# A new order of steps for a fused attention and gated-MLP kernel: two sink exponentials in place of four, two gate tiles begun on half their contraction, and a last tile in halves

## The chip, the cores and the metric

The kernel runs on one core of one Trainium2 chip. The metric is the device time of one execution in microseconds: the median of eight runs of the unchanged kernel, and one more execution under the hardware profiler, from which all lines of profile below come. A core has five engines that run side by side and wait for one another by semaphores: PE (matrix multiply; its weight loads are listed as PEld), DVE (vector), ACT (scalar, with function tables), POOL (GpSimd) and SP (which here only issues transfers). Sixteen DMA engines move data.

## What is computed

Attention with a window of 128 and four sink positions, for 4 batches, 8 heads, 768 positions and 64 dimensions a head; then a gated MLP on the result, with a spatial projection over positions.

```python
scores = scale * np.matmul(q, k.transpose(0, 1, 3, 2))
keep = is_sink | in_window          # pos < 4, or 0 <= row - col < 128
a = softmax(np.where(keep, scores, -1e9))
x = heads_joined(np.matmul(a, v))   # (4, 768, 512)
h = gelu_tanh(x @ w_in)             # (4, 768, 1024)
u, v = h[..., :512], h[..., 512:]
v_n = (v - mean(v)) / np.sqrt(var(v) + 1e-06) * g_ln
v_s = np.einsum('ts,bsd->btd', w_sg, v_n) + b_sg[None, :, None]
out = x + (u * v_s) @ w_out
```

Inputs and output are float32; inside, matrices are bf16 and sums float32.

## The kernel before

Everything is written out as one list of steps by hand, the string STEPS. A step is a name and indices, and the program calls the function of that name; each function issues instructions on fixed engines, and an engine takes its own in the order of the list. There is no scheduler at run time: an instruction that waits holds all that is behind it on its engine. The first index is the batch b. Heads go in pairs p (0 to 3), the 768 positions in six tiles of 128 (t or j).

The steps of attention, with their lines in the kernel before:

- LQ, LK, LV load q, k, v. Pair 0 of batch 0 comes over SP in float32 (`first`, L200) and is cast by CQ and CK (L221); all other loads are issued by POOL (L192, L214), cast on the way. Batch 3's q and k come in rows (L196, two transfers a step) and are turned by transposing DMAs of SP.
- TQ, TK turn q and k of a pair on PE (L300, twelve transposes); EQ, EK copy the result out of PSUM (L219 on ACT, L221 on DVE; the step's last letter names the engine).
- QK.b.p.g computes scores of group g (0 to 2) of a pair (L350), EX their exponential on ACT (L358; 128x1024, or 128x768 for g = 2), MK masks it, on DVE (L365) or in two instructions on POOL (L369, L373).
- KS, SK, SX make the sinks' scores and their exponential (L323, L332 and L336, L341). In batch 0 one SK and one SX are done for each pair, elsewhere one SX for the batch.
- AV.b.p.h averages v for one half h of the positions, tiles 0 to 2 or 3 to 5 (L390 to L400), NR divides by the sum (L409, L410 on DVE). VSM prepares the sinks' v (L288, L289); its data come by LC, four small transfers of SP.
- XT.b.i transposes x (L419; i selects a half of the positions and of the columns: XT.0.0 and XT.0.2 need pairs 0 and 1, XT.0.1 and XT.0.3 pairs 2 and 3), XE copies it out. Batches 2 and 3 use a transposing DMA instead (XD).

The steps of the MLP: MV.b.jj makes two tiles of the value half (L436, eight matmuls over four contraction blocks c), GV its gelu (L440), BN the statistics (L449, L450, L452), RS the power -1/2 on POOL (L457), NM and Z the normalised tile z (L460; L466 on ACT, L469 on DVE). MU.b.i and GU do the gate half (L478, L484). WT and WE turn the spatial weights once (L491, L494); LW loads w_in in two halves, LWS the spatial weights, LWO w_out. SP.b.h.dc is the spatial projection (L499; the step, not the engine), GT adds bias and scale (L504, DVE), GM multiplies by the gate (L509, DVE or POOL). OU.b.t is one output tile (L516, 128x512), RA adds x (L520, DVE), ST stores it (L523, issued by SP). HM.n puts n matmuls without use ahead of the next step on PE[...].

Buffers are rings that a step takes in turn: two score buffers in PSUM shared by QK, MV and MU; four PSUM banks shared by all other PE steps, so that such a step waits for the reader of the fourth one before it; three output tiles ot; three buffers vt. The MLP of a batch is interleaved with the attention of the next. POOL's transfers use eight semaphores in turn: each waits for the landing of the eighth before it.

Of the kernel before, what the change touches and what calls it, by code (L numbers as in the profile page):

```python
# [16 lines left out]
ZERO LQ.0.0 IDEN LK.0.0 LQ.0.1 FILL LK.0.1 LC VSK MASK LV.0.0 MASK0 CQ.0.0.D LQ.0.2 HM.7 TQ.0.0 CK.0.0.D LK.0.2  # L17
EQ.0.0.A TK.0.0 LV.0.1 EK.0.0.A TQ.0.1 KS.0.0 QK.0.0.2 LQ.0.3 EQ.0.1.D QK.0.0.0 EX.0.0.2 SK.0.0 LK.0.3 VSM.0 TK.0.1
LV.0.2 EK.0.1.D SX.0.0 QK.0.0.1 MK.0.0.2.P EX.0.0.0 HM.1 TQ.0.2 KS.0.1 LV.0.3 EX.0.0.1 MK.0.0.0 SK.0.1 QK.0.1.2 LW.0
TK.0.2 EQ.0.2.D SX.0.1 QK.0.1.1 EX.0.1.2 EK.0.2.D MK.0.0.1.P EX.0.1.1 QK.0.1.0 MK.0.1.2.D LW.1 HM.1 AV.0.0.0 EX.0.1.0  # L20
KS.0.2 QK.0.2.1 MK.0.1.1.D TQ.0.3 LWS EX.0.2.1 QK.0.2.0 MK.0.1.0 AV.0.1.1 LWO EX.0.2.0 NR.0.0.0 AV.0.1.0 QK.0.2.2
NR.0.1.1 TK.0.3 EQ.0.3.A MK.0.2.1.P NR.0.1.0 EK.0.3.A SK.0.2 LQ.1.0 AV.0.0.1 MK.0.2.0 SX.0.2 XT.0.0 KS.0.3 LK.1.0
EX.0.2.2 NR.0.0.1 QK.0.3.0 AV.0.2.0 LV.1.0 EX.0.3.0 XE.0.0.D QK.0.3.1 XT.0.2 MK.0.2.2.D EX.0.3.1 SK.0.3 LV.1.1
MK.0.3.0 QK.0.3.2 AV.0.2.1 NR.0.2.0 SX.0.3 MK.0.3.1.P EX.0.3.2 NR.0.2.1 XE.0.2.A LQ.1.1 MK.0.3.2.D HM.1 AV.0.3.0
NR.0.3.0 LK.1.1 AV.0.3.1 LV.1.2 NR.0.3.1 XT.0.1 XE.0.1.A HM.1 XT.0.3 LV.1.3 XE.0.3.D MV.0.0 VSM.1 VSM.3 MV.0.2 GV.0.0
VSM.2 LG WT.3 WT.1 GV.0.2 WE.3 MV.0.1 BN.0.0 MU.0.3 GV.0.1 BN.0.2 WT.2 GU.0.3 MU.0.2 BN.0.1 RS.0.2 WT.4 GU.0.2 WT.5
MU.0.0 NM.0.2 RS.0.1 WE.1 Z.0.5.A WE.2 Z.0.4.A TQ.1.1 WE.4 TQ.1.0 NM.0.1 GU.0.0 WE.5 TK.1.0 LQ.2.0 MU.0.1 Z.0.3.D
Z.0.0.A Z.0.2.D EQ.1.1.A Z.0.1.D WT.0 EQ.1.0.D GU.0.1 SP.0.1.0 EK.1.0.D SP.0.1.2 GT.0.1.0 WE.0 QK.1.0.2 GM.0.1.0.P
# [36 lines left out]

HOLDS = "LG<LWS"


DT = (3,)


@with_exitstack
def kernel(
    ctx: ExitStack,
    tc: tile.TileContext,
# [12 lines left out]
    nc = tc.nc  # L90
# [482 lines left out]
```

## Time and profile before

| | us |
|---|---|
| median of 8 runs | 160.94 |
| lowest and highest run | 160.38, 162.25 |
| the profiled execution | 162.19 |
| its span on the core | 160.5 |
| PE idle before its first instruction | 2.29 |
| first transposes of q on PE | 5.77 |
| first value tile of batch 0 (L436) | 26.97 |
| last matmul ends | 155.81 |

The span is what the profile covers; some 1.7 us of the execution lie around it. Table rows from 2.29 on are read from the timeline, in microseconds from the span's start.

The busy time of each engine in eleven stretches of the span, as the profile sums it (a pair of numbers is busy time and count of instructions; PEclk is the granted clock of PE):

```profile
core 0: us, PE busy (x) PEld busy (x) DVE busy (x) ACT busy (x) POOL busy (x), PEclk, DMA share, GB/s
0.00:6.00 6.00, 3.38 (x13) 1.20 (x15) 3.33 (x16) 1.28 (x1) 5.12 (x14) 1.00 0.72 173
6.00:16.00 10.00, 7.23 (x111) 4.32 (x107) 7.05 (x13) 7.41 (x10) 10.00 (x14) 0.86 1.74 166
16.00:28.00 12.00, 10.53 (x176) 7.04 (x175) 10.36 (x27) 10.57 (x14) 8.36 (x12) 0.97 1.27 206
28.00:42.00 14.00, 14.00 (x133) 8.83 (x132) 12.51 (x32) 10.01 (x13) 4.75 (x5) 1.00 1.54 202
42.00:70.00 28.00, 27.97 (x425) 17.60 (x422) 26.91 (x56) 23.39 (x29) 23.88 (x33) 1.00 1.46 149
70.00:86.00 16.00, 15.28 (x118) 8.32 (x117) 13.78 (x32) 12.48 (x14) 13.92 (x17) 1.00 1.97 179
...
144.00:156.00 12.00, 11.81 (x65) 6.12 (x63) 8.96 (x17) 0.12 (x1) 3.64 (x4) 1.00 0.24 89
156.00:160.50 4.50, 0.00 (x0) 0.00 (x0) 1.18 (x2) 0.00 (x0) 0.00 (x0) 0.95 0.47 175
```

A busy PE is not a PE at its peak, since the ends of pipelined matmuls are modelled. In the stretch from 42 to 70 us four engines are busy for over four fifths of the time; in the last 4.5 us only DVE and the store's transfer work.

### The profile page before, as it was taken

The page shows a single profiled execution, that of the slowest core. Times are in us where ns is not written, and L with a number is a line of the kernel's source. Part 1 is how long each engine was busy: PE and PEld are TensorE (multiplying, and loading weights), DVE is VectorE, ACT ScalarE, POOL GpSimd, SP SyncE. Part 2 cuts the span into 40 slices and gives each one's busy share as a digit, 9 for nine tenths or more (in the row PEclk, how much of TensorE's full clock was granted, in tenths as well). Part 3 has the DMA queues.
Part 4 walks back from the last instruction along what each step waited for, and adds up shares of the span by engine and source line. Part 5 has one row for each costly group of instructions (what it writes and reads, how often), then busy time and mean ns, then how long its engine had stood idle before and what let it go on. Part 6 is the DMA issues. An engine that isn't in the chain of part 4 may idle for free.

```text
span 160.5 us, 3815 instructions
## 1 busy us (share of the span) xinstructions
PE 148.2 (92%) x1519; PEld 86.3 (54%) x1519; DVE 133.2 (83%) x304; ACT 100.9 (63%) x118; POOL 88.9 (55%) x123
## 2 busy tenths in 40 slices
PE   4749997999999999999989999999999999999980
PEld 1325664566565667734655655545756654556530
DVE  4469897699999999998789989779999945887861
ACT  3387997549869869976887749746897024580000
POOL 7999784244257999999992680404045420214400
PEclk9996999999999999999999999999999999999999
DMA  5999999999972999999999989410300890111055
GB/s 172 168 161 172 199 213 206 204 222 185 176 105 17 173 194 273 140 138 119 234 172 191 165 155 179 131 65 0 135 0 0 133 263 0 65 70 63 4 198 196
DMA packets 63122, 22.70 MB, mean 141 GB/s; under 512 B 51456, under 2 KB 59904, under 8 KB 63104
## 3 DMA queue, kind: packets, MB, share of 16 engines
q0 software_dynamic: 45600, 11.80, 76.6%
q1 hardware_dynamic: 17504, 10.66, 27.5%
q8 instruction: 12, 0.20, 0.5%
q14 instruction: 6, 0.05, 0.1%
HBM read 24.81 MB, written 6.29 MB: 194 GB/s over the span
## 4 chain that ended last, share of the span: by engine, by line
PE 75%; POOL 6%; ACT 6%; DVE 4%; DMA 4%; issue 1%; POOLq 0%; DVEq 0%; ACTq 0%
PE mm L499 20%; PE mm L516 11%; PE sc L436 11%; PE sc L478 10%; PE sc L350 7%; PE mm L300 5%; DMA q<-in_q_dram 4%; PE mm L390 3%; ACT P L358 3%; PE mm L396 2%; PE mm L400 2%; DVE z L469 2%; PE mm L419 1%; PE mm L491 1%; POOL v_sb L214 1%
## 5 line engine op out<-in xcount | busy, mean ns | idle before, releaser
L358 ACT ACTIVATE P<-sc 128x1024 bf16<-128x1024 f32 (+1 forms) x48 | 43.9, 959 | 9.1 <-PE sc L350 9.0
L499 PE MATMUL mm<-wsgT,z 128*128 128x384 bf16 x192 | 34.7, 327 | 0.7 <-DVE z L469 0.7
L499 PEld LDWEIGHTS <-z 128*128 128x128 bf16 x192 | 17.6, 98 | 13.4 <-issue 2.1
L509 POOL TENSOR_TENSOR wsg_gated<-gtmp,uT 128x384 bf16<-128x384 bf16 x15 | 14.1, 947 | 18.1 <-DVE gtmp L504 18.1
L478 PE MATMUL sc<-xT,w_in_sb 128*128 128x384 bf16 x128 | 23.1, 326 | 0.0
L516 PE MATMUL mm<-w_out_sb,wsg_gated 128*128 128x512 bf16 x96 | 22.7, 379 | 0.0
L369 POOL TENSOR_SCALAR_AFFINE_SELECT P<-P 128x512 bf16<-128x512 bf16 x20 | 13.3, 663 | 16.4 <-ACT P L358 16.3
L436 PE MATMUL sc<-w_in_sb,xT 128*128 128x512 bf16 x96 | 22.0, 379 | 0.0
L504 DVE SCALAR_TENSOR_TENSOR gtmp<-mm,g_sb,b_bc 128x384 bf16<-128x384 f32 x32 | 19.4, 612 | 2.4 <-PE mm L499 2.3
L365 DVE TENSOR_TENSOR P<-P,mask 128x1024 bf16<-128x1024 bf16 (+1 forms) x28 | 20.8, 756 | 0.4 <-ACT P L358 0.2
L520 DVE TENSOR_TENSOR ot<-mm,x_sb 128x512 f32<-128x512 f32 x24 | 16.1, 686 | 5.0 <-PE mm L516 4.7
L449 DVE BATCH_NORM_STATS2 st<-vt 128x6 f32<-128x512 f32 x24 | 16.2, 673 | 4.7 <-ACT vt L440 4.7
L214 POOL DMA_DIRECT2D v_sb<-in_v_dram x16 | 16.5, 1038 | 5.4 <-DMA wsg_gated<-in_moe_w_sg_dram 4.3
L484 ACT ACTIVATE uT<-sc 128x768 bf16<-128x768 f32 x16 | 12.7, 802 | 10.1 <-PE sc L478 10.1
L440 ACT ACTIVATE vt<-sc 128x1024 f32<-128x1024 f32 x12 | 12.3, 1023 | 10.5 <-PE sc L436 10.5
L410 DVE TENSOR_TENSOR x_sb<-mm,rcp 128x384 bf16<-128x384 f32 x32 | 17.8, 558 | 1.1
L390 PE MATMUL mm<-v_sb,P 128*128 128x65 bf16 x192 | 17.2, 196 | 0.7 <-ACT xT L219 0.6
L457 POOL TENSOR_TENSOR rs<-rs,neg_half 128x2 f32<-128x2 f32 (+1 forms) x8 | 7.0, 875 | 18.4 <-DVE rs L452 15.7
L390 PEld LDWEIGHTS <-P 128*128 128x128 bf16 x192 | 14.8, 99 | 4.4 <-issue 2.6
L350 PE MATMUL sc<-qT,kT 64*128 64x256 bf16 x192 | 16.3, 272 | 0.8 <-ACT kT L219 0.8
L478 PEld LDWEIGHTS <-w_in_sb 128*128 128x128 bf16 x128 | 12.3, 98 | 8.5
L396 PE MATMUL mm<-v_sb,P 128*128 128x65 bf16 x160 | 16.0, 195 | 0.0
(73 smaller groups left out, 231.0 us busy)
## 6 DMA issues: line engine op xcount, KB each, us to landing
out_dram<-ot SPq DMA_DIRECT2D x24, 256.0 KB, 2.4
v_sb<-in_v_dram POOLq DMA_DIRECT2D x16, 192.0 KB, 8.2
q<-in_q_dram POOLq DMA_DIRECT2D x4, 384.0 KB, 12.5
k<-in_k_dram POOLq DMA_DIRECT2D x4, 384.0 KB, 11.9
wsg_gated<-in_moe_w_sg_dram POOLq DMA_DIRECT2D x1, 1152.0 KB, 14.1
w_in_sb<-in_moe_w_in_dram POOLq DMA_DIRECT2D x2, 512.0 KB, 9.0
qn<-in_q_dram POOLq DMA_DIRECT2D x8, 96.0 KB, 6.9
kn<-in_k_dram POOLq DMA_DIRECT2D x8, 96.0 KB, 6.5
```

Of the source, the lines that this page charges most:

```text
L214: return nc.gpsimd.dma_start(out=v_sb[b % len(v_sb)][:, 2 * p:2 * p + 2, :, 0:Dh].rearrange("p h t d -> p (h t) d"), in_=v[b, 2 * p:2 * p ...
L350: nc.tensor.matmul(sc[:, hl, 256 * jl:256 * jl + n], kT[b, p][rows, 128 * j:128 * (j + 1)], qT[b, p][rows, 128 * j:128 * j + n], start=Tru ...
L358: nc.scalar.activation(out=pt[:, :, 0:w], in_=sc_ring[b, p, g][:, :, 0:w], func=AF.Exp, scale=scale)
L365: nc.vector.tensor_mul(pt[:, :, 0:w], pt[:, :, 0:w], m.unsqueeze(1).to_broadcast([128, 2, w]))
L390: nc.tensor.matmul(av[:, il, hl, :], P[b, p, i // 2][:, hl, 256 * (i % 2):256 * (i % 2) + 128], vb[:, h, i, :], start=first, stop=False)
L396: nc.tensor.matmul(av[:, il, hl, :], P[b, p, j // 2][:, hl, 256 * (j % 2) + 128:256 * (j % 2) + 256], vb[:, h, j, :], start=False, stop=False)
L410: nc.vector.tensor_mul(xs[:, 3 * half:3 * half + 3, 128 * p:128 * (p + 1)].rearrange("p t (h d) -> p t h d", h=2), av[:, :, :, 0:Dh], rcp. ...
L436: nc.tensor.matmul(hp[:, jl, :], xT[b][:, j, c, :], w_in_sb[:, c, d_half:2 * d_half], start=(c == 0), stop=(c == KD - 1))
L478: nc.tensor.matmul(hp[:, n, 0:NH], w_in_sb[:, c, 128 * dc:128 * (dc + 1)], xT[b][:, 3 * hf:3 * hf + 3, c, :], start=(c == 0), stop=(c == K ...
L499: nc.tensor.matmul(ps[:, 0:NH], z[b][:, si, 128 * dc:128 * (dc + 1)], wsgT[:, si, NH * hf:NH * (hf + 1)], start=(si == 0), stop=(si == NT ...
L504: nc.vector.scalar_tensor_tensor(out=gtmp.new((b, hf, dc)), in0=mm_ring["g", b, hf, dc][:, 0:NH], scalar=g_sb[:, dc:dc + 1], in1=b_bc[:, N ...
L516: nc.tensor.matmul(ps, gatedT[:, (2 * b + hf) % 3, dc, 128 * tl:128 * (tl + 1)], w_out_sb[:, dc, :], start=(dc == 0), stop=(dc == KU - 1))
```

## The change

1. In batch 0 the sinks of two pairs are put into one bank (two SK matmuls, the second adding to the first), so SX is done for pairs 0 and 1 together (SX.0.1) and for 2 and 3 (SX.0.3).
2. MV.0.0 and MU.0.0 are each split over the contraction: MA.0.0 and UA.0.0 do its first two blocks, which need pairs 0 and 1 alone; the rest follows under the old name.
3. q and k of pair 2 of batch 0 are loaded ahead of the first v, pair 3 behind one v in place of two. The casts CQ and CK move from DVE to ACT. The first q and k land in vt buffers; the ring f32 goes, and the rings qT and kT grow from six to eight.
4. Output tile 5 of batch 3 is made, added and stored in two halves of 256 columns (OU, RA, ST, then OB, RB, SB).
5. The whole list of steps is another one: other orders on every engine, and other engines for some masks, copies and products. The functions also gain forms that this list does not use (a turn by rows on PE, TURN "R"; a WE by DMA).

| batch: instruction | before, by engine | after |
|---|---|---|
| 0: masks MK | DVE 8, POOL 4 | DVE 9, POOL 3 |
| 1: masks MK | DVE 7, POOL 5 | DVE 9, POOL 3 |
| 1 and 2: copies EQ | ACT 3, DVE 5 | ACT 6, DVE 2 |
| 0 and 1: copies XE | ACT 4, DVE 4 | ACT 2, DVE 6 |
| 1: products GM | DVE 4, POOL 4 | DVE 5, POOL 3 |
| 2: z | ACT 2, DVE 4 | ACT 1, DVE 5 |
| 3: products GM | DVE 4, POOL 4 | DVE 2, POOL 6 |
| all: HM matmuls | 11 | 10 |

```diff
-    f32 = Ring("f32", 2, [128, 2, NT, Dh], F32)
-    qT = Ring("qT", 6, [128, S], BF16)
-    kT = Ring("kT", 6, [128, S], BF16)
+    qT = Ring("qT", 8, [128, S], BF16)
+    kT = Ring("kT", 8, [128, S], BF16)
...
     def SK(b, p0):
-        ps = fresh(mm_ring, ("s", b, p0))
         ks = ks_sink[b % 2]
         if b == 0:
-            nc.tensor.matmul(ps, ks[:, 128 * p0:128 * (p0 + 1)], qT[b, p0][:, 256:768], start=True, stop=True)
+            ps = mm_ring["s", b, p0 - 1] if p0 % 2 else fresh(mm_ring, ("s", b, p0))
+            nc.tensor.matmul(ps, ks[:, 128 * p0:128 * (p0 + 1)], qT[b, p0][:, 256:768],
+                             start=(p0 % 2 == 0), stop=(p0 % 2 == 1))
             return
...
-        e = exs[b, 0 if b else p]
+        e = exs[b, 0 if b else p | 1]
...
+    def MA(b, jj):
+        fresh(sc_ring, ("v", b, jj))
+        v_part(b, jj, range(KD // 2))
+
+    def MV(b, jj):
+        if ("v", b, jj) in sc_ring.held:
+            return v_part(b, jj, range(KD // 2, KD))
+        fresh(sc_ring, ("v", b, jj))
+        v_part(b, jj, range(KD))
...
+    def UA(b, i):
+        fresh(sc_ring, ("u", b, i))
+        u_part(b, i, range(KD // 2))
...
+    def cols_of(b, t, second=False):
+        n = d_model // 2 if b == B - 1 and t in LAST else d_model
+        return slice(n, 2 * n) if second else slice(0, n)
...
+    def OB(b, t):
+        o_part(b, t, cols_of(b, t, True))
```

The order in the places that the prediction speaks of, before and after. POOL at the start:

```diff
-LQ.0.1 LK.0.1 VSK MASK LV.0.0 LQ.0.2 LK.0.2 LV.0.1 LQ.0.3 LK.0.3 LV.0.2 MK.0.0.2.P LV.0.3 LW.0 MK.0.0.1.P LW.1 LWS LWO
+LQ.0.1 LK.0.1 MASK LQ.0.2 VSK LK.0.2 LV.0.0 LQ.0.3 LK.0.3 LV.0.1 LV.0.2 LV.0.3 LW.0 LW.1 LWS LWO
```

PE at the end of the first batch:

```diff
-AV.0.2.1 AV.0.3.0 AV.0.3.1 XT.0.1 XT.0.3 MV.0.0 MV.0.2 WT.3 WT.1 MV.0.1
+AV.0.3.0 AV.0.2.0 XT.0.2 MA.0.0 AV.0.3.1 XT.0.1 AV.0.2.1 UA.0.0 MV.0.0 MU.0.0 XT.0.3 MV.0.1 WT.3 WT.5
```

POOL around the powers of batch 1:

```diff
-LK.3.0 LV.3.0 MK.2.0.2.P LQ.3.1 LK.3.1 LV.3.1 MK.2.1.2.P LQ.3.2 RS.1.2 LK.3.2 LV.3.2 LQ.3.3 RS.1.1 LK.3.3 LV.3.3
+LQ.3.0 LK.3.0 LV.3.0 MK.1.3.1.P LQ.3.1 MK.1.2.1.P MK.2.0.1.P LK.3.1 MK.2.0.2.P MK.2.1.1.P LV.3.1 LQ.3.2 LK.3.2 LV.3.2 LQ.3.3 RS.1.2 LK.3.3 LV.3.3 RS.1.1
```

PE at the end:

```diff
-SP.3.0.1 SP.3.1.1 SP.3.0.0 SP.3.0.3 SP.3.1.0 SP.3.0.2 SP.3.1.2 SP.3.1.3 OU.3.1 OU.3.2 OU.3.0 OU.3.4 OU.3.3 OU.3.5
+SP.3.0.3 SP.3.0.0 SP.3.0.1 SP.3.1.2 SP.3.0.2 SP.3.1.3 SP.3.1.0 OU.3.0 OU.3.1 SP.3.1.1 OU.3.2 OU.3.5 OU.3.3 OB.3.5 OU.3.4
```

## The prediction, made before the changed kernel ran

> **What bounds the kernel now.** First the page: busy times, then the forty slices (4.01 us each), then the chain.
>
> ```profile
> PE 148.2 (92%) x1519; PEld 86.3 (54%) x1519; DVE 133.2 (83%) x304; ACT 100.9 (63%) x118; POOL 88.9 (55%) x123
> PE   4749997999999999999989999999999999999980
> DVE  4469897699999999998789989779999945887861
> DMA  5999999999972999999999989410300890111055
> ```
>
> TensorE is the bound from slice 8 (28 us) to slice 39 (156 us). Before that it waits, and only there and at the end can much be won. DVE is as full between 40 and 73 us. The DMA engines are full until 44 us. Busy PE time is modelled at its ends, so I price PE steps from start to start in the chain: a value tile (L436) 1.73 us, a gate tile (L478) 1.30, a spatial tile (L499, six matmuls) 0.97, an output tile (L516) 0.86. Comparing each step's start-to-start time with the quickest quarter of its kind, PE loses 3.9 us in all after 27 us: 2.1 between 42 and 70 us, 1.1 between 70 and 86 us (0.9 of it one wait at SP.1.1.3, 83.2 us), some 0.7 later.
>
> Next the timeline of the first batch (start, duration, operation, idle time before it and what ended it).
>
> ```profile
> 9.76 1.95 ACT L358 ACTIVATE P<-sc 128x1024 bf16<-128x1024 f32 x2
> 12.99 0.60 ACT L341 ACTIVATE exs<-mm 128x512 bf16<-128x512 f32 x1 [1.28 <-PE mm L332]
> 10.48 0.93 DVE L289 TENSOR_TENSOR v_sink<-vs,headsel 128x512 bf16<-128x512 f32 x1 [1.18 <-DMA vs<-in_v_dram]
> 12.10 0.36 PEld L300 LDWEIGHTS <-q 128*64 128x64 bf16 x12 [2.23 <-DMA q<-in_q_dram]
> 23.41 0.88 ACT L358 ACTIVATE P<-sc 128x768 bf16<-128x768 f32 x1
> 26.97 3.40 PE L436 MATMUL sc<-w_in_sb,xT 128*128 128x512 bf16 x15
> ```
>
> ACT has one long stop (11.71 to 12.99 us), then runs nearly without one until the last exponential ends at 24.29; the last masks, averages, divisions and transposes follow it, and the first value tile starts at 26.97. The third q pair lands only at 12.1 us; its queue had one v load ahead of it.
>
> Third, the chain of waits around 70 to 86 us, and the end.
>
> ```profile
> 75.36 0.72 POOL rs L457
> 76.08 1.68 POOL kn L196 x2
> 77.76 1.01 POOL v_sb L214
> 78.78 1.64 POOL qn L196 x2
> 80.42 1.07 POOL rs L457
> 81.50 0.17 DVE nmr L460
> 81.70 2.68 DVE z L469 x3
> ...
> 142.83 7.80 PE mm L499 x48
> 150.63 5.19 PE mm L516 x24
> ```
>
> The second power of batch 1 stands on POOL behind five loads' issues; its z are late, and SP.1.1.3 waits. The end is eight spatial tiles and six output tiles with no gap; the last two additions (DVE L520, 0.69 each) follow, and the last store.
>
> [...] the same 128x1024 mask takes 0.68 us, or 1.11 (at 51.08) under POOL's work. [...]
>
> **The change part by part.**
>
> Two sink exponentials go: 2 x 0.49 us (start to start, 19.95 to 20.44) on ACT, about 1.0. But CQ and CK come to ACT. They are unseen there: below by DVE's 0.70[...]; I take 0.80. They run at 3.85 and 5.6 us, when q and k land (3.83, 5.58) and ACT is idle until 6.64, so they cost nothing; DVE is rid of 1.5 us.
>
> I walked the new order through the first batch with these rows. EK.0.0 starts at about 7.05, the first exponential at 8.6 as before. VSM.0 still stands on DVE ahead of EK.0.1 and still waits for the 10.4 us landing, so EK.0.1 ends at 12.3 and the next exponential starts at 12.75: ACT stops for 2.2 us here, not 1.28. From there ACT has six wide exponentials (0.92), four narrow (0.70), two sink ones, two copies and XE.0.2: 5.5+2.8+1.0+1.4+0.7 = 11.4. It is never starved in my walk if q.3 lands by 15 us (15.3 before; with two v loads behind it, about 13.8), so the last exponential ends near 23.3 instead of 24.29. The v loads come later (the last near 19.4) but AV.0.3.0 is first asked for at 22.2.
>
> MA (half of 1.73 = 0.86) and UA (half of 1.30 = 0.65) need half 0 of pairs 0 and 1 only, and the weights, landed at 21.34 and 23.88. They run at about 23.6 and 25.9, where PE would wait for the divisions of pairs 2 and 3. The second half of MV.0.0 then starts at 26.55, with 1.51 us done in advance and only XT.0.3 (0.35) still open. Before stood there at 26.97 with nothing done: 26.97 - 26.55 + 1.51 - 0.35 = 1.6 us gained. An unmodelled slip of 0.3 (contention, landings) leaves 1.3. The warm-up matmul less (0.2) lies in waiting time. What is late next: batch 1's first q landed at 35.17 and nothing ahead of it in the queue shrinks; PE arrives there near 34.9. So not much more can be kept.
>
> Batch 1, 40 to 67 us. EQ moves from DVE to ACT three times (0.86 off DVE, 0.70 on ACT each), two masks come from POOL to DVE (0.61 each), XE and a product join DVE. Summed over the list from GT.0.1.0 to the last mask of batch 2's first pairs, DVE has 25.4 us where before had 26.3 (which took 29.9 with contention); ACT has 23.5 for 22.3. POOL has two masks less, but LQ.3.0, LK.3.0 and LV.3.0 (1.65+1.65+1.03) stand ahead of MK.1.3.1: it ends near 57.7, AV.1.3.0 is asked for at 57.9. Each buffer of the ring of four is free in time in my walk, and PE loses 0.35 us where it lost 2.1: 1.7 gained. DVE's contention was 3 us; the walk has only 1.5 us of DVE idleness to hide it, so I give back 0.9 and take 0.8.
>
> The z of batch 1. From MV.1.0 the new PE order has 3x1.73+4x1.30+3x0.86 and 2.5 us of averages and scores before SP.1.1.0: 15.4 us. LQ.3.2 to LQ.3.3 are issued before the first power; the second still has LK.3.3 and LV.3.3 ahead (1.65+1.03). BN.1.1 ends about 11.0 after MV.1.0 starts, the power at 13.1, the last z at 14.9, or 15.4 with DVE under contention (the three took 2.68 against 1.6). That just fits, so most of the 0.9 goes: I take 0.4.
>
> Stages of batch 2 and 3 up to 143 us have the same work and the wait that could open (XD.3.1, landed 3 us ahead before) has 1.6 us left: nothing.
>
> The end. SP.3.1.1 now stands last, behind OU.3.0 and OU.3.1, with its product on POOL. Before, SP.3.1.3 ended at 150.63, its GT at 151.36 and its product (POOL) at 152.35: with 0.06 to PE 1.78 us, under three output tiles (2.6). Now OU.3.2 (0.86) and one half-width matmul (0.11) cover it: a stop of 0.81. Against that, RA.3.4 no longer waits behind RA.3.5: one addition (0.69) after the last matmul, not two. Tail: 157.18 - 142.83 = 14.35 before; 13.0 + 0.81 + 0.73 = 14.5: +0.2. Halving tile 5 shortens nothing that ends last.
>
> Sum: -1.3 - 0.8 - 0.4 + 0.2 = -2.3 us. The profiled execution took 162.19 (span 160.5, 1.7 around it): about 159.9, span 158.2. It lies 1.25 above the median; on the median of 160.94 the forecast is 158.6.
>
> **The rivals.**
>
> DVE stays the second bound: batch 1 waits as before and the z too. For it: its row of nines from 40 to 73, and masks at 1.1 us. Against: 0.9 us less on its list. Gain 1.3 - 0.2 = 1.1: 159.8.
>
> The transfers set the start: batch 1's q and k land no earlier, so a PE that arrives earlier waits at TQ.1.0, or LV.0.0 and q.3 come later than I take and hold AV.0.0.0 and TQ.0.3. For it: the DMA row, and only 0.3 us between arrival and landing. Against: before lost nothing there. First batch gains 0, the rest 1.0: 159.9. Both rivals at once, so that only the end counts: about 161.
>
> Slower: ACT becomes the bound of batch 1. The place is its two score buffers: MV.1.0 needs EX.2.1.2. ACT's list up to it is 21.4 us from 42.0, which gives 63.4; PE comes at 65.1 if it never waits. In before, ACT idled 4.5 us in this stretch, waiting for scores between copies. My forecast has MV.1.0 at about 66.7 (40.0 for the first spatial tile, 25.8 of work and stops, 0.9 given back), so it holds gaps up to 3.3 us; beyond that each costs one. At 5.6 us the gain of 2.3 is gone, and that is the point from which it decides; at 7 it takes 162.3. Against it: batch 1's scores are asked for earlier than ACT reaches them in my walk.
>
> That the edits don't act at all is excluded for the exponentials (ACT has two less) but not for MA and UA: if XE.0.0 comes late they only push AV.0.3.1 back. That is within the second rival.
>
> **How the numbers follow.** Forecast 55%, one of the first two rivals 22%, both 11%, slower 12%. The forecast's own range is 157.3 to 159.7 (batch 1 winning from 0.2 to the walk's 1.7, the z from 0 to 0.9, the first batch from 0.8 to 1.6). 0.5% is 0.8 us, about what a measurement of this kernel can tell from no change. Faster by that: 0.55 + three quarters of 0.22 = 0.72; within: 0.05 + 0.10 = 0.15; slower: 0.12 + 0.01 = 0.13. For 8 in 10 the range reaches from 157.0 to 161.3.
>
> **What would show it.** Right: two sink exponentials in batch 0, and the two f32 copies done on ACT before 6.6 us; the first half value tile before 24.5 us; the last exponential of batch 0 near 23.3; PE idle under 0.5 us before the first batch-1 spatial tile; no z wait above 0.4 us; and a new stop of about 0.8 us before the half-width output tile. Wrong: batch-1 transposes of q waiting for a DMA; DVE or ACT ending PE's waits for more than 2 us in 40 to 70 us.

## The result, and the profile after

The changed kernel took 160.48 us (median of 12 runs), the kernel before, run beside it, 161.33 (33 runs): 0.85 us less. The ratio, 0.992 [0.989, 0.996] or 1.3 us less, is taken without the slow runs (three of the 12 were), and it is this number that is used below. The forecast was 2.3 us less. The direction holds; about half of the gain, or somewhat more, is missing. The two profiled executions differ by 2.67 us (162.19 and 159.52), more than the medians: the one lies 1.25 us above the median of the eight runs shown ahead of the prediction, the other 0.96 below the 160.48. The first thing to see is what sets them apart. The top of the page of the kernel after, busy times and three rows of slices:

```profile
PE 146.7 (93%) x1522; PEld 86.7 (55%) x1522; DVE 128.2 (81%) x305; ACT 100.6 (64%) x118; POOL 86.9 (55%) x118
PE   4878889989999999999999999999999999999970
PEclk9999999999999999999999999999999999999998
DMA  5999999999999999999999059431000591030154
```

Beside it the clock row of the kernel before, which the prediction did not read, and three stretches of its profile (busy time and count by engine; the last three columns are the granted clock, DMA share and GB/s):

```profile
PEclk9996999999999999999999999999999999999999
```

```profile
12.00:13.27 1.27, 1.16 (x21) 0.69 (x23) 1.24 (x3) 0.28 (x1) 1.27 (x2) 1.00 1.39 186
13.27:16.68 3.41, 3.41 (x38) 1.81 (x38) 3.34 (x7) 2.96 (x4) 3.41 (x6) 0.50 2.09 171
16.68:20.00 3.32, 3.12 (x72) 2.40 (x71) 2.93 (x8) 3.27 (x5) 2.45 (x5) 1.00 1.31 200
```

In the profiled execution of before, PE ran at half clock for 3.41 us inside the first batch. Ahead of that, q of pair 2 had landed late, at 12.06 us (at 10.66, 11.56 and 11.79 in three later profiles with the same first batch and whole clock). The forecast took its first batch (first value tile at 26.97 us) from this execution and carried the difference to the median.

Now the places that the prediction named, in the kernel after. ACT in the first batch (timeline: start, duration, operation, idle time before it and what ended it), and TensorE at batch 1's first q:

```profile
8.52 1.96 ACT L366 ACTIVATE P<-sc 128x1024 bf16<-128x1024 f32 x2
11.41 1.02 ACT L366 ACTIVATE P<-sc 128x1024 bf16<-128x1024 f32 x1 [0.94 <-PE sc L358]
...
20.85 1.52 ACT L366 ACTIVATE P<-sc 128x768 bf16<-128x768 f32 x2
```

```profile
33.56 0.50 PE L519 MATMUL mm<-iden,wsg_gated 128*128 128x128 bf16 x6
34.67 0.86 PE L304 MATMUL mm<-iden,q 128*64 128x128 bf16 x24 [0.61 <-DMA q<-in_q_dram]
```

The last exponential ends at 22.37 (forecast 23.3) and the second half of MV.0.0 starts at 25.33 (26.55), so the first batch is earlier than forecast. ACT stops for 0.94 us at 11.41, where the walk had 2.2: VSM.0 starts its product at 9.36 us, when the sinks' v has landed, not at 10.48 as before. But TQ.1.0 then stands: from start to start WT.2 takes 0.77 us longer than its usual 0.34, until q has landed at 34.62. The chain of waits of the same execution goes through this landing and not through the first batch:

```profile
13.48 0.74 POOL w_out_sb L242
14.23 20.40 DMA q<-in_q_dram
...
34.67 0.86 PE mm L304 x24
```

The wait for z is gone; the three rows are of POOL, DVE and PE (second power, z, first matmuls of SP.1.1.0). SP.1.1.0 starts without a stop:

```profile
78.82 1.07 POOL L475 TENSOR_TENSOR rs<-rs,neg_half 128x4 f32<-128x4 f32 x1
...
80.12 1.46 DVE L487 TENSOR_SCALAR z<-vt,rs,nmr 128x512 bf16<-128x512 f32 x3
...
82.25 0.65 PE L529 MATMUL mm<-wsgT,z 128*128 128x384 bf16 x3
```

And the end, POOL's last product and the output tiles behind it:

```profile
150.34 0.91 POOL L539 TENSOR_TENSOR wsg_gated<-gtmp,uT 128x384 bf16<-128x384 bf16 x1 [3.80 <-DVE gtmp L534]
...
151.31 0.93 PE L545 MATMUL mm<-w_out_sb,wsg_gated 128*128 128x256 bf16 x5 [0.86 <-POOL wsg_gated L539]
```

From here on two numbers are used for each kernel. "Start to start" is the time from the first matmul of one step to that of the next; what lies above the lower quartile for that kind of step, over both profiles, is called loss. From SP.0.1.0 to the first of the eight last spatial tiles, before took 102.08 us and after 99.94, of which 0.66 is a QK and a TK that after does ahead of SP.0.1.0. The other 1.48 is loss that went: before lost 2.81 us from 41 to 68 us, 2.31 from 68 to 101 and 0.81 from 101 to 145; after lost 2.57, 1.11 and 0.75. From that first tile to the end of the span before took 17.8 us and after 18.0.

So the 2.67 us between these two executions are 1.4 in the first batch (SP.0.1.0 starts 0.75 earlier, with 0.66 of work done ahead), 1.5 of loss, and 0.2 given back at the end. Between the two profiles, then, the first batch gains what was forecast for it. The question for the runs below is whether it does in other executions.

### The profile page after: what moved, and what is told of

It reads as the page before. It is cut to its first block, busy times and chain, and to the rows that moved or that the text cites. A ratio compares the mean times of both kernels' runs of the same rounds, so it can differ in the third digit from the quotient of the medians.

```text
span 157.8 us, 3835 instructions
## 1 busy us (share of the span) xinstructions
PE 146.7 (93%) x1522; PEld 86.7 (55%) x1522; DVE 128.2 (81%) x305; ACT 100.6 (64%) x118; POOL 86.9 (55%) x118
## 3 DMA queue, kind: packets, MB, share of 16 engines
q1 hardware_dynamic: 17648, 10.66, 28.2%
## 4 chain that ended last, share of the span: by engine, by line
PE 67%; DMA 13%; POOL 8%; DVE 7%; issue 1%; POOLq 1%; DVEq 0%
PE mm L529 19%; DMA q<-in_q_dram 13%; PE mm L545 12%; PE sc L496 12%; PE sc L444 10%; PE sc L358 5%; PE mm L398 3%; PE mm L304 3%; POOL v_sb L216 3%; DVE P L373 2%; PE mm L404 2%; DVE gtmp L534 2%; PE mm L408 1%; POOL q L194 1%; POOL k L194 1%; DVE x_sb L418 1%
## 5 line engine op out<-in xcount | busy, mean ns | idle before, releaser
L529 PE MATMUL mm<-wsgT,z 128*128 128x384 bf16 x192 | 34.2, 326 | 0.0
L529 PEld LDWEIGHTS <-z 128*128 128x128 bf16 x192 | 17.8, 98 | 12.2 <-issue 1.3
L545 PE MATMUL mm<-w_out_sb,wsg_gated 128*128 128x512 bf16 (+1 forms) x100 | 23.7, 371 | 0.9 <-POOL wsg_gated L539 0.9
L534 DVE SCALAR_TENSOR_TENSOR gtmp<-mm,g_sb,b_bc 128x384 bf16<-128x384 f32 x32 | 19.4, 612 | 4.5 <-PE mm L529 3.3
L444 PE MATMUL sc<-w_in_sb,xT 128*128 128x512 bf16 x96 | 22.5, 379 | 0.1
L553 DVE TENSOR_TENSOR ot<-mm,x_sb 128x512 f32<-128x512 f32 (+1 forms) x25 | 16.5, 665 | 7.3 <-PE mm L545 7.2
L373 DVE TENSOR_TENSOR P<-P,mask 128x1024 bf16<-128x1024 bf16 (+1 forms) x31 | 21.6, 713 | 0.4 <-ACT P L366 0.2
L377 POOL TENSOR_SCALAR_AFFINE_SELECT P<-P 128x512 bf16<-128x512 bf16 x17 | 11.1, 656 | 19.0 <-ACT P L366 12.7
L539 POOL TENSOR_TENSOR wsg_gated<-gtmp,uT 128x384 bf16<-128x384 bf16 x16 | 15.4, 966 | 11.1 <-DVE gtmp L534 11.0
L475 POOL TENSOR_TENSOR rs<-rs,neg_half 128x4 f32<-128x4 f32 (+1 forms) x8 | 7.0, 879 | 21.3 <-DVE rs L470 19.4
L418 DVE TENSOR_TENSOR x_sb<-mm,rcp 128x384 bf16<-128x384 f32 x32 | 17.8, 558 | 1.1
L358 PE MATMUL sc<-qT,kT 64*128 64x256 bf16 x192 | 15.3, 263 | 2.8 <-ACT P L366 1.5
L496 PEld LDWEIGHTS <-w_in_sb 128*128 128x128 bf16 x128 | 12.3, 98 | 9.0
L398 PEld LDWEIGHTS <-P 128*128 128x128 bf16 x192 | 14.7, 98 | 4.4 <-issue 2.2
L398 PE MATMUL mm<-v_sb,P 128*128 128x65 bf16 x192 | 16.5, 194 | 0.3
L404 PE MATMUL mm<-v_sb,P 128*128 128x65 bf16 x160 | 15.5, 193 | 0.0
```

Source lines behind the costliest of these rows:

```text
L358: nc.tensor.matmul(sc[:, hl, 256 * jl:256 * jl + n], kT[b, p][rows, 128 * j:128 * (j + 1)], qT[b, p][rows, 128 * j:128 * j + n], start=Tru ...
L373: nc.vector.tensor_mul(pt[:, :, 0:w], pt[:, :, 0:w], m.unsqueeze(1).to_broadcast([128, 2, w]))
L398: nc.tensor.matmul(av[:, il, hl, :], P[b, p, i // 2][:, hl, 256 * (i % 2):256 * (i % 2) + 128], vb[:, h, i, :], start=first, stop=False)
L404: nc.tensor.matmul(av[:, il, hl, :], P[b, p, j // 2][:, hl, 256 * (j % 2) + 128:256 * (j % 2) + 256], vb[:, h, j, :], start=False, stop=False)
L418: nc.vector.tensor_mul(xs[:, 3 * half:3 * half + 3, 128 * p:128 * (p + 1)].rearrange("p t (h d) -> p t h d", h=2), av[:, :, :, 0:Dh], rcp. ...
L444: nc.tensor.matmul(hp[:, jl, :], xT[b][:, j, c, :], w_in_sb[:, c, d_half:2 * d_half], start=(c == 0), stop=(c == KD - 1))
```

## The experiments

Every run was timed against the kernel before on the same chip. The first four were expected from two theories. Theory 1, the clock: the forecast's first-batch gain is the difference to an execution with a halved clock. Theory 2, the steps: the gain is there, and steps behind it give it back.

**The kernel before, unchanged.**

> The unchanged kernel, profiled once more. Theory 1 (the clock): the execution profiled before had PE's clock at 0.5 from 13.3 to 16.7 us, and this, not the order of steps, made up over 1 us of its first batch; so an execution whose clock is 1.0 there has a span of about 159.0, the first value tile near 25.5 us, and ends 160.7. Theory 2 (the steps): the old order costs this much at any clock; span 160.5, first value tile near 27.0. If the clock is halved in the first 20 us again, the profile is as before under both. Ratio to before 1.000.

Measured: ratio 1.000 [0.997, 1.003]. Its profiled execution (span 162.0) had half clock from 12.0 to 18.8 us, and its first value tile came at 28.45 us; so it doesn't decide between the theories. In the four microseconds ahead of that (first row: 8 to 12 us), PE was busy for 1.66 us:

```profile
8.00:12.00 4.00, 1.66 (x25) 0.86 (x26) 2.24 (x5) 3.13 (x4) 4.00 (x6) 1.00 1.50 152
12.00:18.80 6.80, 6.11 (x68) 3.55 (x69) 6.42 (x11) 4.26 (x5) 4.96 (x7) 0.50 1.74 182
```

**Before, with eight matmuls without use ahead of TQ.0.2.**

```diff
-HM.1 TQ.0.2
+HM.8 TQ.0.2
```

> The unchanged kernel with eight warm-up matmuls in place of one ahead of TQ.0.2, where PE waits for q (9.8 to 12.1 us). They fit into the wait (8 x 0.22 = 1.7 us). Theory 1 (the clock is halved after a stretch in which PE is mostly idle): few or no executions have a clock under 0.99, the median is about 160.7, ratio 0.994 to 0.998, and the first value tile starts near 25.5 us. Theory 2 (the steps): as before, 161.3, ratio 1.000; the first value tile near 27.0.

Measured: ratio 0.999 [0.995, 1.002]; the clock is whole in the profile, and yet the first value tile comes at 26.25 us, not near the 25.5 of theory 1: q of pair 2 landed at 11.56, and from that landing to the tile it is 14.69 us, against 14.91 in the first profile of before. 13 of 14 executions have a mean clock of 0.993 or more, against 28 of 42 of the unchanged kernel. Where the kernel before has such a clock its median is 160.86; here it is 161.24. So a whole clock alone brought nothing in the median; what takes its gain back is not shown (in the profile the last extra matmul ends at about the time at which q lands). And of what before's first profile was later than this one, 0.72 us, the landing of q makes 0.50.

**The old first batch, with the new rest.** The list of before up to XE.0.3 (with its four sink exponentials, v ahead, casts on DVE), then that of the changed kernel, halved last tile included.

> The old list up to XE.0.3 of batch 0 (four sink exponentials, v ahead of q and k, whole tiles), then the changed kernel's list, with the last tile in halves. Theory 1: the later stages gain little at equal clock (up to 0.6) and the end loses 0.1 to 0.2: ratio 0.996 to 1.001. Theory 2 (the forecast's own terms, -1.2 and +0.2): ratio 0.993 to 0.995.

Measured: 160.0 us, ratio 0.992 [0.989, 0.996]: as much as the whole change, without its first batch. Its profile (clock 1.0, span 158.3) has the first value tile at 25.03 us, and TQ.1.0 stands for q here too:

```profile
35.13 0.86 PE L304 MATMUL mm<-iden,q 128*64 128x128 bf16 x24 [0.47 <-DMA q<-in_q_dram]
```

The two spans, 157.8 and 158.3, differ by as much as the two starts of TQ.1.0, 34.67 and 35.13: from there both run the same steps in the same time.

**The new first batch, with the old rest.** The reverse, last tile whole.

> front_only once more with GU.0.0 directly behind MU.0.0: the changed kernel's first batch (two sink exponentials, MA and UA, q and k ahead of v, casts on ACT) and behind it the order of the kernel before, whole last tile. Forecast of the prediction: the first batch alone is worth 1.3 us (ratio 0.992). Theory 'clock': the forecast took the first batch of before from an execution in which PE's clock was halved from 13.3 to 16.7 us; against executions without that the new first batch reaches the same point 0.86 us earlier at most, and the old list of batch 1 gives part of that back: ratio 0.995 to 1.0. Theory 'transfers': the old list asks for batch 1's q only 2.7 us after its landing, so here no transfer can hold what the first batch gains, and the ratio should be 0.995 or less at an unhalved clock.

Measured: ratio 1.009 [1.005, 1.012], clock 1.0 in its profile: slower than before. (A first form, in which GU.0.0 stood behind MV.0.1, so that one gelu read a buffer already overwritten, gave 1.003 [0.999, 1.007].) The sewn list has its own losses: MV.0.1 starts at 32.90 us, TQ.1.1 only at 39.14. It doesn't tell what the first batch is worth. But it showed something else: its second half of MV.0.0 began at 27.02, although its last exponential had ended at 22.78, only 0.41 later than in the changed kernel (where that half began at 25.33).

**w_out behind batch 1's first q and k.** The same edit in the changed kernel and in rest_only.

```diff
-LWS LWO LQ.1.0 LK.1.0 LV.1.0
+LWS LQ.1.0 LK.1.0 LWO LV.1.0
```

> The changed kernel with one load moved: LWO (w_out, 2.5 us of landing, first used by an output tile near 54 us) goes behind batch 1's first q and k on POOL's queue. In the changed kernel's profile TQ.1.0 stood 0.61 to 0.77 us until that q landed at 34.62; in the kernel with the old first batch and the new rest (rest_only) it stood 0.47 until 35.08, and the two profiled spans differ by the difference of these landings. Theory 'transfers': q lands near 32.1, the wait goes, PE starts TQ.1.0 near 33.9, SP.0.1.0 near 39.1 (39.84 in the changed kernel), and the span is 0.6 to 0.9 us shorter: ratio to before near 0.987, profiled span near 157.0. Theory 'later waits': the wait goes, but batch 1's scores, powers or products are late instead, MV.1.0 stays at 66.8 and the time at the changed kernel's (ratio 0.992).

> rest_only (first batch of the kernel before, everything after it of the changed kernel) with the same move of LWO behind batch 1's first q and k. Theory 'transfers': TQ.1.0's wait of 0.47 goes, the span is about 0.35 to 0.6 us shorter than rest_only's 158.3, and now the old first batch is 0.6 to 0.9 us behind the new one (a_qfirst), which it was not with LWO ahead (ratios 0.9923 and 0.9922): ratio to before near 0.990. Theory 'later waits': no difference to rest_only and none to a_qfirst.

Measured: 159.77 (ratio 0.990 [0.986, 0.994]) and 159.79 (0.992 [0.987, 0.996]). q lands at 31.24 and 31.95, and the wait is gone in both. The row of a_qfirst that answers to the 0.61 above has no stop in it:

```profile
34.97 0.86 PE L304 MATMUL mm<-iden,q 128*64 128x128 bf16 x24
```

But PE comes there at 34.97, no earlier than where it stood before (in this execution at half clock from 12.71 to 16.13 us), and the two first batches still are not told apart by the medians. So the transfer looks like one gate and not the only one.

**The last product on DVE.**

```diff
-GM.3.1.1.P
+GM.3.1.1.D
```

> The changed kernel with one step on another engine: GM.3.1.1, the product that the last output tiles wait for, on DVE in place of POOL. POOL's took 0.91 us (150.34 to 151.25) and the half-width tile OU.3.5 stopped for 0.61 us behind it. A product on DVE takes about 0.4 to 0.5: the stop shrinks to 0.1 to 0.2 us and the last addition ends about 0.45 us after the changed kernel's distance from SP.3.0.3 (14.3 in place of 14.76 us): ratio near 0.989. If the stop is another one (the adjacent GT on DVE, or a PSUM bank), the distance stays at 14.7 and the ratio at 0.992.

Measured: 159.64, ratio 0.988 [0.984, 0.992]. DVE and PE at the end:

```profile
150.97 0.36 DVE L539 TENSOR_TENSOR wsg_gated<-gtmp,uT 128x384 bf16<-128x384 bf16 x1
...
151.39 0.93 PE L545 MATMUL mm<-w_out_sb,wsg_gated 128*128 128x256 bf16 x5 [0.20 <-DVE wsg_gated L539]
```

The stop falls from 0.86 to 0.20 us, and from SP.3.0.3 to the end of the span the kernel takes 17.4 us, not 18.0: a little more than the 0.46 expected. Its first batch has the changed kernel's order, and yet the second half of MV.0.0 began at 26.70, not 25.33, at a clock of 1.0. What differs in its profile is POOL.

**The changed kernel once more, and POOL's masks ahead of batch 1's loads.** The prediction had not looked at what stands on POOL between the loads of the first batch and its first mask. The change put LQ.1.0, LK.1.0 and LV.1.0 there. LV.1.0 waits for the landing of the eighth transfer before it, LV.0.2 (v of pair 2), the ninth of POOL's transfers in both orders: its issue starts 0.28 or 0.29 us after that landing in three profiles (16.36 and 16.64 in the changed kernel, 17.64 and 17.92 in a_gmd, 18.55 and 18.84 in a_again). In the kernel before, MK.0.2.1.P stood ahead of these three issues and waited for its exponential alone:

```profile
17.82 0.63 POOL L369 TENSOR_SCALAR_AFFINE_SELECT P<-P 128x512 bf16<-128x512 bf16 x1 [0.87 <-ACT P L358]
```

```diff
-LWS LWO LQ.1.0 LK.1.0 LV.1.0 MK.0.2.1.P MK.0.3.1.P LV.1.1 LQ.1.2 MK.0.3.2.P LK.1.2
+LWS LWO MK.0.2.1.P MK.0.3.1.P LQ.1.0 LK.1.0 MK.0.3.2.P LV.1.0 LV.1.1 LQ.1.2 LK.1.2
```

> The changed kernel once more, beside the kernels that differ from it in one thing. Both theories: ratio 0.990 to 0.994; the second half of MV.0.0 starts 12.3 to 13.8 us after AV.0.0.0 (12.34 in its first profile, 13.60 and 13.79 in two other kernels with the same first batch), and TQ.1.0 starts at the landing of batch 1's q.

> The changed kernel with POOL's masks of pairs 2 and 3 ahead of batch 1's first loads, w_out still ahead of these in the transfers. Theory 'POOL': the second half of MV.0.0 starts 12.5 us after AV.0.0.0 (12.55 in both kernels that had this order), but TQ.1.0 stands until q's landing near 34.6 to 35.4, so little of it arrives: ratio 0.989 to 0.992. If POOL's issues alone ate the gain, the ratio falls to 0.986 or less and no wait at TQ.1.0 is left; if they play no part, the 12.3 to 13.8 remain and the ratio is a_again's.

> a_masks once more, for its profile. Theory 'POOL': POOL's first mask starts within 0.9 us of its exponential's end whatever the v loads' landings, DVE's two masks beside it take 1.4 us (1.39, 2.43 and 3.51 us in three profiles with the loads ahead), the second half of MV.0.0 starts 12.5 us after AV.0.0.0, and TQ.1.0 then stands at the landing of batch 1's q for 0.3 to 1.0 us. If the loads ahead play no part, the distance is 13 us or more.

Measured: a_again 160.21 us, 0.987 [0.981, 0.993]; a_masks 159.70, 0.986 [0.981, 0.991]; a_masks2, the same kernel, 159.84, 0.993 [0.989, 0.996]. In time this edit alone can't be told from nothing. (The profiled execution of a_masks took 248.2 us, at 0.57 of the clock, and can't be compared.) The profiles show how the edit acts, each in one execution. The timelines of the changed kernel (first profile), of a_again and of a_masks2, with POOL's issue of LV.1.0 (a v_sb load), its first mask, DVE's two masks beside it, and in a_again the average on PE that waits for them:

```profile
16.64 1.02 POOL L216 DMA_DIRECT2D v_sb<-in_v_dram  x1 [0.52 <-DMA v_sb<-in_v_dram]
17.66 0.65 POOL L377 TENSOR_SCALAR_AFFINE_SELECT P<-P 128x512 bf16<-128x512 bf16 x1
```

```profile
18.84 1.02 POOL L216 DMA_DIRECT2D v_sb<-in_v_dram  x1 [1.65 <-DMA v_sb<-in_v_dram]
19.86 0.65 POOL L377 TENSOR_SCALAR_AFFINE_SELECT P<-P 128x512 bf16<-128x512 bf16 x1
19.88 3.51 DVE L373 TENSOR_TENSOR P<-P,mask 128x1024 bf16<-128x1024 bf16 x2
...
22.29 0.27 PE L398 MATMUL mm<-v_sb,P 128*128 128x65 bf16 x3 [0.74 <-DVE P L373]
```

```profile
17.46 0.63 POOL L377 TENSOR_SCALAR_AFFINE_SELECT P<-P 128x512 bf16<-128x512 bf16 x1 [2.99 <-ACT P L366]
...
19.63 1.38 DVE L373 TENSOR_TENSOR P<-P,mask 128x1024 bf16<-128x1024 bf16 x2
```

Where v of pair 2 lands late, POOL's masks come late, fall together with DVE's, and DVE's two then take 3.51 us, not 1.39. In a_again the first of POOL's masks stood behind the issue of LV.1.0 until 19.86, though its exponential had ended near 17.6 (an estimate from the changed kernel, where it ended at 17.58 and that row of exponentials began 0.04 us earlier, at 14.90). In the order of a_masks2 POOL waits for ACT alone. The four profiles beside one another (us):

| | v of pair 2 lands | first POOL mask | DVE's two masks | last exponential ends | second half of MV.0.0 |
|---|---|---|---|---|---|
| changed kernel | 16.36 | 17.66 | 1.39 | 22.37 | 25.33 |
| a_gmd | 17.64 | 18.95 | 2.43 | 22.48 | 26.70 |
| a_again | 18.55 | 19.86 | 3.51 | 22.42 | 28.43 |
| a_masks2 | 17.86 | 17.46 | 1.38 | 22.17 | 25.34 |

(In a_masks2 the first matmul of that half has no record; 0.65 us after UA.0.0, as in the other three, it would be at 25.13.) ACT is done at the same time in all four. The rest goes with the landing, until the masks are moved ahead of the loads: then a landing at 17.86 costs nothing. (In a_again PE also ran at half clock from 22.9 to 26.3 us, so not all of its 3.1 us is the masks'.) And in a_masks2 what is won stands at the next gate, the row of PE:

```profile
34.88 0.86 PE L304 MATMUL mm<-iden,q 128*64 128x128 bf16 x24 [0.76 <-DMA q<-in_q_dram]
```

**Both gates opened.** a_qfirst's order of w_out and the masks ahead, and then the small stops too.

> a_qfirst (w_out behind batch 1's first q and k) with POOL's two masks of pairs 2 and 3 ahead of batch 1's first loads, and the third mask ahead of LV.1.0, LV.1.1 and LQ.1.2. In a_gmd's profile, whose first batch is that of the changed kernel, POOL's issues of LQ.1.0, LK.1.0 and LV.1.0 stood 0.52, 0.91 and 0.52 us (landings of earlier transfers, a read of the buffer); its first mask came at 18.95 us, not 17.66 as in the changed kernel's profile, fell together with DVE's masks (two took 2.43 us, not 1.39), the last mask came 1.45 later, and the second half of MV.0.0 began at 26.70, not 25.33. Theory 'POOL': the spread of the first batch and the loss of the forecast 1.3 us come from these issues ahead of the masks; now POOL's first mask starts within 0.3 us of its exponential's end (near 16.9), the second half of MV.0.0 begins near 25.2 in any execution at full clock, SP.0.1.0 near 38.9, ratio to before 0.984 to 0.987. Theory 'transfers alone': nothing changes against a_qfirst (ratio 0.990, SP.0.1.0 near 40.2).

Measured: 159.23, ratio 0.987 [0.982, 0.992]; from AV.0.0.0 to the second half of MV.0.0 12.3 us (counted from UA.0.0, as in a_masks2). SP.0.1.0 came at 40.79, not at 38.9: in this execution PE had turned pair 1's k only by 11.2 us (by 9.4 in the changed kernel's), and its clock was halved from 8.7 to 12.1 us. The absolute times of the expectation failed (the second half was expected near 25.2, and came near 26.95), the distance and the upper end of the ratio held; the intervals of q_masks and a_qfirst overlap.

```diff
-VSM.0 ... EK.0.1.D ... EQ.0.2.D
+EK.0.1.D ... EQ.0.2.D VSM.0
-GM.3.1.1.P
+GM.3.1.1.D
```

> q_masks and two more moves: VSM.0 behind the copies EK.0.1 and EQ.0.2 on DVE (it waits for the sinks' v near 10 us and held EK.0.1, so ACT stood 0.94 us until 11.41), and GM.3.1.1 on DVE. Theory 'POOL' with the stop of ACT: the exponential after the stop starts near 10.8, everything up to the first value tile is 0.5 to 0.6 us earlier than in q_masks, PE idles less before 12 us, so that the clock is halved in fewer executions; the tail is 0.65 us shorter (a_gmd: 12.51 us from SP.3.0.3 to OU.3.4, 13.16 in the changed kernel). Ratio to before 0.977 to 0.981, about 157.5 us. If the first batch is held elsewhere, only the tail shows: 0.65 us below q_masks.

Measured: 158.97, ratio 0.985 [0.980, 0.989]; span 157.1. The tail is right (17.4 us). Of the other 0.5 to 0.6 us little is left: ACT's stop before the third exponential falls from 0.94 to 0.34, but KS.0.1 now waits behind VSM.0, SK.0.1 behind it for 0.76, and ACT stands 0.58 there. So the ratio misses the 0.977 to 0.981 that was expected. None of its six executions shows a mean clock under 0.996.

Beside the profile of the changed kernel (span 157.8) nearly all of the 0.7 us is the tail: SP.0.1.0 starts at 39.73, there at 39.84. So against that execution the opened gates gain next to nothing. In the medians best lies 1.2 to 1.5 us below the changed kernel's two (160.48 and 160.21), of which the tail makes 0.6; that the rest comes from executions like those of a_gmd and a_again becoming rare fits the profiles, and is not shown.

**Two parts undone, in that kernel.** MA and UA away; and the four sink exponentials back.

```diff
-MA.0.0 ... UA.0.0
-SX.0.1 ... SX.0.3
+SX.0.0 SX.0.1 ... SX.0.2 SX.0.3
```

> best without MA and UA: MV.0.0 and MU.0.0 whole, as in the kernel before. The prediction counted 1.51 us of work done in advance in waiting time. If that is right, MV.0.1 starts 0.9 to 1.5 us later than in best and the ratio rises by 0.006 to 0.009. If those halves only push back AV.0.3.1 and AV.0.2.1, which run behind them, the difference is under 0.4 us.

> best with four sink exponentials in batch 0 again, one for each pair with its own bank. The prediction counted about 1.0 us of ACT time (2 x 0.49) on the path to the last exponential. If ACT sets the first batch, the last exponential ends and MV.0.1 starts 0.8 to 1.0 us later than in best and the ratio rises by 0.005 to 0.006; if masks and averages set it, by less than 0.002.

Measured: best_nosplit 160.54, ratio 0.994 [0.991, 0.996]; best_4sx 159.17, 0.987 [0.982, 0.992]. Both profiles show the same first steps as best (TQ.0.2, with the warm-up matmul ahead of it, at 9.76 in best_nosplit and 9.75 in best; in best_4sx at 9.15, so its steps are counted from there). Without MA and UA, MV.0.1 starts at 28.77, not 28.04: 0.73 us, less than the 0.9 to 1.5 expected, half of the 1.51 that the forecast counted. A further 1.0 us is lost between SP.0.1.0 and MV.1.0 (28.03 us against 27.03), most of it at one average, AV.1.0.1 (0.92 above its usual time, 0.29 in best), where PE stands 0.76 us for one of DVE's masks; why that follows from a start 0.74 later was not tried. In the medians the whole is 1.57 us and the ratio 0.009 higher, so by the time alone the 1.51 would look confirmed; the profile shows only half of it where the forecast had it. With four exponentials the last one ends 0.97 us later, counted from the third, as forecast (11.63 and 12.60), but MV.0.1 only 0.35 us later counted from TQ.0.2: masks and averages that follow on DVE and POOL take up the rest.

**v ahead of q and k again; and two steps more.**

```diff
-LQ.0.2 LK.0.2 LV.0.0 LQ.0.3 LK.0.3 LV.0.1 LV.0.2 LV.0.3
+LV.0.0 LQ.0.2 LK.0.2 LV.0.1 LQ.0.3 LK.0.3 LV.0.2 LV.0.3
```

> best with the first batch's v loads ahead of q and k of pairs 2 and 3, as in the kernel before. q of pair 2 lands 1.5 to 2.5 us later (near 12, 9.68 in best), PE stands before TQ.0.2, and its clock is halved in more executions. If this order is worth what the prediction gave it (the last exponential near 23.3, not 24.29, of which the exponentials made 1.0), nothing is lost at full clock; if the earlier q is what keeps ACT and the clock going, the ratio is 0.990 or more (best: 0.9845) and over a quarter of the executions show a clock under 0.993.

Measured: 160.30, ratio 0.989 [0.983, 0.994]. Three of six executions have a clock under 0.993, and the median of the other three is 159.19, close to best's 158.97; in its profile (clock 1.0) q of pair 2 lands at 10.17 us, no more than 0.5 after best's, though 1.5 to 2.5 was expected. So at full clock the order of loads shows no effect on the steps here; whether it keeps the clock up is suggested by three executions against none of six, and by no more.

```diff
-EK.0.1.D ... KS.0.1 ... MV.0.0 MU.0.0 XT.0.3 MV.0.1
+EK.0.1.D KS.0.1 ... MV.0.0 XT.0.3 MU.0.0 MV.0.1
```

> best with two steps moved: KS.0.1 directly behind EK.0.1 on DVE (in best SK.0.1 stood 0.76 us for it, and ACT 0.58 for SK.0.1) and XT.0.3 directly behind the second half of MV.0.0, ahead of MU.0.0's (MV.0.1 stood 0.29 us for the copy of XT.0.3). Expected: MV.0.1 starts 0.5 to 0.9 us earlier than in best from the same point TQ.0.2 (18.29 us in best), ratio 0.980 to 0.982, near 157.9 us. If the stops only move to the masks, 18.0 to 18.3 and the ratio of best (0.9845).

Measured: 158.99, ratio 0.982 [0.977, 0.986], span 157.1: best's time. MV.0.1 starts 18.15 us after TQ.0.2 (18.29 in best), so the second case of the expectation holds: the stops moved to DVE's masks (AV.0.0.0 stands 0.44 us for one). These two kernels, near 159.0 us, are the fastest measured: the changed kernel had 160.48 and 160.21, and 159.64 with its last product moved.

## Why the forecast was half right

**The first batch, -1.3 us: this is the step that failed.** With old and new first batch ahead of the same rest, the ratios are 0.992 and 0.992, and with w_out moved 0.992 and 0.990: between nothing and about 0.3 us (by the intervals, an estimate, each uncertain by some 0.9, so that the 1.3 lies just outside). Against its own profile the step came true, which was luck in the choice of executions: one of before with a late q and a half clock, one of after with an early landing of v. Three parts of that step went wrong.

- The sentence on the v loads, that they "come later (the last near 19.4) but AV.0.3.0 is first asked for at 22.2", looked for the data's reader only. The reader that mattered was POOL's queue: LV.1.0 waits for the landing of the eighth transfer before it, LV.0.2 (16.36 to 18.55 us), and the change had put MK.0.2.1.P, which stood ahead of LQ.1.0 in before, behind LV.1.0 (MK.0.3.1.P stood behind it in both). The forecast counted landings here, and not issues. It costs from nothing to 1.4 us at full clock (25.33 and 26.70), by how late a transfer lands in that execution.
- The time started from, 26.97, belongs to an execution with a late landing of q and then half clock for 3.41 us, and was carried to a median in which most executions have no such stretch. At full clock the same old first batch reaches its value tile at 25.03 (rest_only), 25.99 (r_qfirst) and 26.25 (b_warm), 14.2 to 14.7 us after q of pair 2 has landed; in before it was 14.91. So of the 1.94 us between 26.97 and 25.03 the landing makes 1.40, and the rest is left for the clock (against r_qfirst 0.27 of 0.98, against b_warm 0.50 of 0.72). New, with its work done ahead taken off as in the prediction (1.51 - 0.35), it is 24.17, 25.54 (a_gmd) and about 23.97 (a_masks2). Counted from AV.0.0.0, old takes 11.54, 11.37 and 11.37 us and new, in the changed kernel, 11.18 (12.34 less that work): what new gains in these profiles lies mostly ahead of AV.0.0.0, at the landings.
- The sizes, as undone in best: at MV.0.1, MA and UA are worth 0.73 us, not 1.51 of work in waiting time; the two exponentials 0.35, not 1.0. The walk let everything that ACT gains pass to PE. (Its sum for ACT is also a little off: 12.75 + 11.4 is 24.15, or 23.45 without XE.0.2, which comes after the last exponential; 23.3 was carried on. CQ and CK, put at 0.80 us by an estimate for which before shows DVE's 0.70 alone, took 0.83 each on ACT, at 3.91 and 5.31; nothing rests on that.)

**The second rival, transfers set the start,** was named with its place, TQ.1.0, and its wait is in three profiles (0.61 us in the changed kernel, 0.47 in rest_only, 0.76 in a_masks2). By its parts (first batch 0, rest 1.0) it is the case that came nearest to what was measured. But it doesn't look like the whole cause: with this gate open (a_qfirst) the first batch's gain still did not show. That the two gates stand in series is read from the profiles; in the time, opening one alone or both (q_masks, 159.23) gives intervals that overlap, and only with the tail mended as well (best, 158.97) does the kernel stand about clear of the changed one. The prediction had seen this gate ("PE arrives there near 34.9. So not much more can be kept") and yet left the 1.3 standing.

**Batch 1, -0.8: 0.24 found** (up to 0.5 if the stretch is cut at the same steps and not at the same times). MV.1.0 starts at 66.81 (forecast 66.7), but the stretch also began earlier, at 39.84 (forecast 40.0). The loss of the kernel after was put at 0.35 + 0.9 against 2.1; found are 2.57 against 2.81, in pieces under 0.3 us. The first rival, DVE as second bound, has this small gain (its other part, the z waiting as before, did not come). But the waits of PE that the profile puts down to DVE from 42 to 70 us fall from 1.6 to 0.6 us, so what keeps the rest is open.

**The z, -0.4: 0.9 found, and 1.2 in the whole stretch.** The walk was right to a tenth: the power ended 13.08 us after MV.1.0 began (forecast 13.1), the last z at 14.77 (14.9), PE came at 15.44 (15.4). Only the cut for contention was wrong: the three z on DVE took 1.46 us, not the 2.68 of before, and it was not needed.

**The end, +0.2: +0.2.** The stop was 0.86 us (forecast 0.81), and one addition in place of two gave most of it back. The prediction did not ask what the product costs on DVE: 0.36 us against POOL's 0.91.

**The rest as a sum** was forecast at -1.0; rest_only measured 0.992 of 161.04, which is -1.2 [-1.8, -0.7]. The slower rival (ACT as the bound of batch 1) did not come up: in 42 to 70 us no wait of PE of note ends on ACT.

## What to carry to other kernels

When loads are reordered, look at what each transfer's issue waits for and at what stands behind it in its engine's queue, besides the reader of the data (in a_again LV.1.0 stood 1.65 us on POOL for the landing of the eighth transfer before it, and the masks behind it). Before a stage of a profile is subtracted from, read the clock row over that stage, and start from an execution that is like the median one. Where several gates stand in series, opening one may show nothing in the time (here a_masks's 0.986 against a_again's 0.987); the trace has to say which gate comes next, and the test is to open both together.

## What the runs showed of the hardware

- In these profiles the clock of PE fell to half for 3.41 us (6.83 in b_again) after a stretch in which PE was partly idle. The changes of the clock in a profile lie a multiple of 3.41 us apart (in before at 6.44, 13.27 and 16.68 us). Cut into windows of that length, from its first change to 150 us, the 18 profiles other than a_masks's have 747 windows at whole clock; six of them were followed by half clock, with PE busy for 1.17 (b_again), 1.48 (before), 1.76 (q_masks), 1.94 (a_again) and 1.95 us (a_qfirst, and front_only, the first form of front_only2). In the 741 others PE was busy for 2.0 us or more, but for one with 1.91 (r_qfirst). So here the border lies near 1.9 to 2.0 of 3.41 us, by busy times whose ends are modelled. What it costs here: of the unchanged kernel's 42 executions beside b_again, 14 had a mean clock under 0.993, with a median of 162.5 us against 160.9.
- Two DVE masks of 128x1024 took 1.39, 2.43, 3.09 (front_only2) or 3.51 us where POOL's masks lay beside them for 0.24, 1.88, 2.10 or 2.85 us: 2.5 times as long at worst, while POOL's own grew from 0.64 to 1.09 only in its last piece. The prediction knew a single one at 1.11 (51.08 us); POOL was issuing loads beside it (50.15 to 52.19), as it was beside one of 0.68 at 19.56, so what slowed that one is not shown.
- The landing of one and the same load in the first batch shifts by over 2 us between executions (v of pair 2: 16.36 to 18.55), although all are issued at 9.20; everything from SP.0.1.0 to the last eight spatial tiles took 99.93 to 100.00 us in eleven of the thirteen comparable profiles with the new rest (best_4sx 100.17, best_nosplit 100.99).
